# Fetching back and twinning rows of gradients one row per transfer, in parts, in a backward kernel whose end is set by DMA traffic

## The chip, the cores and the metric

The kernel runs on one core of a Trainium2 chip. The metric is device time in microseconds (us). Three timed runs gave 458.6 to 459.25 us, median 459.16. One further execution was profiled: it took 458.38 us, of which the profile's span, from the first to the last instruction of the program, covers 456.6 us.

## The reference, cut to what matters

A one-token decoder network of two block kinds, A (attention over the last 4096 positions of a cache) and B (a dense layer with the mish activation), is run as A, B, A, B with the same weights in both repetitions. The kernel returns the output and the gradients of everything but a bias input that is held constant.

```python
x = A_x                                            # [1, 1, 1024], bf16
x = x + A(layernorm(x), k_cache, v_cache, wq, wo)  # q = x@wq (32 heads of 128, 4 kv heads), softmax over the last 4096 keys, @wo
x = x + B(layernorm(x), w1, b1, w2)                # h = x@w1 + b1 ; h*tanh(softplus(h)) @ w2, inner size 3584
x = x + A(layernorm(x), ...)                       # the same weights again
x = x + B(layernorm(x), ...)
out, vjp = jax.vjp(f, A_x, k_cache, v_cache, wq, wo, w1, b1, w2)
return out, *vjp(grad_out)                         # dk and dv are [1, 4, 32768, 128]: zero but for the last 4096 positions
```

Each weight gradient is a sum of two outer products, one for each repetition (l = 0 and l = 1): for dwo, for example, `dwo[r, c] = oc0[r]*ga0[c] + oc1[r]*ga1[c]`.

## The kernel before, in words

All work is on one core. SyncE (SP in the profile) issues the loads of weights and caches and the stores of the weight gradients; GpSimd (POOL) issues the 56 stores of zeros, 1 MB each, that fill the unused parts of dk and dv (`zeros(n, after)`: POOL first copies one element of a result, so that the n stores start when that result is there). ScalarE (ACT) issues a few small stores. An engine issues in program order.

The forward pass reads the weights as columns. The backward pass goes from block B1 through A1, B0 and A0, and in each block computes the gradient of the block's input. Big weights come through a ring of eight 1 MB slots (`Ring`, line 38): `want` queues a load, and `pump` (line 71 issues it on SP) starts the next one when a slot is released. At the end of B0's backward, `ring.lend(lent)` (line 1119) adds three 1 MB pieces of the tile `W1` that are no longer needed, and the next three loads of wo go there at once. In the profile, tiles whose names begin with W and a number are written `W`, so `W<-W` is a copy inside the tile `W1`.

The weight gradients are made from rows, not columns. The tile `W1` is reused for this: `ROWS` is 128 partitions by 5120 elements of which four pairs of partitions are used, at bases 0, 32, 64 and 96, one pair for each weight gradient (partition base + l for repetition l). Each row holds 1024 elements of one factor and then 3584 or 4096 elements of the other. The columns get there in three ways:

- `rowize` (line 978): TensorE transposes the columns, ACT copies them to SBUF, and for each l one SP transfer (line 986) lays 8 or 32 pieces of 256 bytes into one row. It is called for GB (base 96), GA (base 32) and DQC (base 0). `rowize_f` does the same for DHC (base 64) in 7 pieces of 1024 bytes (line 828).
- `put_by` writes four sets of columns (OC, NA, NB, AC) to small DRAM tensors during the forward pass.
- `take_back` (line 784) fetches them back into `ROWS` in `dn_b0` after its third chunk, at t == 2: one SP transfer for each of the four, 2 rows of 28, 8, 32 and 8 pieces of 256 bytes (line 786). In program order they stand behind `rowize(GB)` and ahead of `rowize_f` and of the three loads of wo that `lend` starts.

`twins` (line 1012), called in the last attention backward at t == 4, copies each pair of rows to a second tile, `TWIN`, at base XOR 32, with one SP transfer for each pair (line 1014): 2 rows of 9216 or 10240 bytes. The twin lets `unit_dw` (line 1016) run the two halves of a 1024-wide unit in two row groups of TensorE. Twins are used only once PSUM has been regrouped in four 1024-wide tiles (`wide`), after the last block's backward.

From there on `work` takes units in turn from four queues: a unit is one or two matmuls of two rows each, an eviction by VectorE (DVE) or ACT (`evac`, lines 305 and 308, which engine by a running sum of costs) into a 1 MB staging buffer, and a store by SP (lines 996 and 1001) when a buffer, or half of one, is full.

Completion of the SP and ACT transfers is counted on eight semaphores that are used in turn (100, 102 to 106, 109 and 110 in the trace). A transfer waits, ahead of its issue, until the earlier transfer on its semaphore has landed.

Of the kernel before, what the change touches and what calls it, by code (L numbers as in the profile page):

```python
# [15 lines left out]
P = 128  # L16
# [77 lines left out]
def kernel(  # L94
# [22 lines left out]
    nc = tc.nc  # L117
# [76 lines left out]
    for hi in range(4):  # L194
        r = slice(32 * hi, 32 * hi + 32)
# [587 lines left out]

    def take_back(name, base, off):
        r = DR[name][:].rearrange("(n l) p -> l n p", l=2)
        nc.sync.dma_start(ROWS[base:base + 2, off:off + r.shape[1] * P].rearrange("l (n p) -> l n p", p=P), r)

    x3, st3, sA1 = attn_fwd(1, x2, st2, False, wo_hook1, last_da)
    put_by("OC", OC, HQ)
# [50 lines left out]
    def dn_b0(g):  # L840
        bcast(lambda c: DHC[:, c, 0:1], STAY)
        mv_open()
        for t in range(TD):
            rowdot(W1[:, t, 0:STAY * P], [LB[0][:, 0:512]], 512, dnp[:, t:t + 1], True)
            mv(W1[:, t, STAY * P:], TF - STAY, TP[:, t:t + 1], lambda i: DHC[:, STAY + i, 0:1], True)
            if t == 2:
                rowize(GB, TD, 96, 0)
                take_back("AC", 96, NOFF)
                take_back("NB", 64, 0)
                take_back("OC", 32, NOFF)  # L850
                take_back("NA", 0, 0)
            if t == 4:
                rowize_f()
        return ln_bwd(dnp, sB0["n32"], sB0["rstd"], g, "B0", lambda k: turn_ahead(("o", 3, 0), ((0,), (1, 2))[k]))
# [110 lines left out]
    ROWS = W1S[:, 0:5120]  # L965
# [7 lines left out]
    TWIN = W1S[:, 11264:16384]  # L973
# [37 lines left out]

    def twins():
        for base, n in ((96, NOFF + F), (64, NOFF + F), (32, NOFF + J), (0, NOFF + J)):
            nc.sync.dma_start(TWIN[base ^ 32:(base ^ 32) + 2, 0:n], ROWS[base:base + 2, 0:n])

    def unit_dw(base, lo, ro, dst, left):

# [135 lines left out]
    def dn1(t):  # L1153
        if t in (3, 6, 7):
            zeros(2 if t == 3 else 1, dnp[:, t:t + 1])
        if t == 4:
            twins()
        if t == 5:
            todo[0].append(units_cols(0, 8, out_4))
# [58 lines left out]
```

## Time and profile before

| | |
|---|---|
| median of three runs | 459.16 us (458.6 to 459.25) |
| the profiled execution | 458.38 us; its span 456.6 us |
| moved by DMA | 183.56 MB, mean 402 GB/s over the span |
| busy share | PE 71%, DVE 56%, ACT 45%, POOL 8% |
| SP's four fetches (line 786) | issued from 280.43 to 282.94 us |
| SP's four twin copies (line 1014) | issued from 321.08 to 327.04 us |
| first eviction from a `wide` tile | 338.70 us |
| last SP store issued | 446.5 us |

Times inside the span are given from its start. In the profile's timeline a row of SP (`SPq`) shows when an issue began and how long SP was held by it; the transfer itself runs later on the core's 16 DMA engines. "DMA share" is the mean busy share of these engines in a stretch. Besides these views, the packed trace holds a record of each DMA packet (start, duration, bytes, queue, but not the engine) and of each semaphore increment by a landing transfer; a time in the text that is said to be from packet or landing records is read there.

### The profile page before, as it was taken

What the parts mean: (1) busy time and instruction counts of PE and PEld (TensorE: products, weight loads), DVE (VectorE), ACT (ScalarE), POOL (GpSimd) and SP (SyncE); (2) the same over time, 40 slices, a digit from 0 to 9 for tenths busy, and PEclk for the clock granted to TensorE, in tenths of its full rate; (3) what the DMA queues carried; (4) which work ended last, traced back from release to release, by engine and by line L of the source; (5) the groups of instructions that cost most, each with busy time, mean ns of one, the idle gap of its engine ahead of it and who ended that gap; (6) DMA issues with size and microseconds to landing.
All of it is one profiled execution on the core that took longest, in us unless ns stands there. A gap on an engine that the chain in (4) does not pass through costs nothing.

```text
span 456.6 us, 13914 instructions
## 1 busy us (share of the span) xinstructions
PE 322.4 (71%) x6225; PEld 258.9 (57%) x6225; DVE 257.5 (56%) x506; ACT 204.6 (45%) x239; POOL 38.5 (8%) x84
## 2 busy tenths in 40 slices
PE   3836543456698898987798868988978988899000
PEld 3735433456597897987798768976922222345000
DVE  4504737278441265846286556763769999989000
ACT  2501001011054277752283542761669999998000
POOL 1000000002031222102100001022130000000000
PEclk9955555555555599978598555995955555555555
DMA  8999999989999999999999979999999999999995
GB/s 334 421 421 421 417 421 419 420 317 422 421 417 423 419 415 416 393 416 418 421 423 425 417 284 342 390 391 420 421 417 420 416 421 419 424 421 418 407 408 227
DMA packets 28377, 183.56 MB, mean 402 GB/s; under 512 B 3706, under 2 KB 3734, under 8 KB 9494
## 3 DMA queue, kind: packets, MB, share of 16 engines
q1 hardware_dynamic: 20162, 123.94, 66.6%
q0 software_dynamic: 8064, 58.72, 31.1%
q8 instruction: 48, 0.79, 0.6%
q14 instruction: 11, 0.09, 0.0%
q10 hardware_dynamic: 92, 0.02, 0.0%
HBM read 83.94 MB, written 98.62 MB: 400 GB/s over the span
## 4 chain that ended last, share of the span: by engine, by line
PE 37%; DMA 28%; DVE 11%; ACT 10%; issue 6%; SPq 0%; ACTq 0%; DVEq 0%
DMA ring<-in_B_w_dram 13%; PE BIG L452 9%; PE TP L471 5%; DMA ring<-in_A_wq_dram 5%; DMA W<-in_A_wo_dram 4%; DMA W<-in_B_w_dram 4%; ACT ring L308 4%; PE wide L1073 4%; PE wide L1022 3%; DVE junk L429 3%; DMA W<-in_A_k_cache_dram 2%; ACT W L308 2%; PE BIG L628 2%; PE MV L648 2%; ACT KT L308 2%
## 5 line engine op out<-in xcount | busy, mean ns | idle before, releaser
L308 ACT COPY ring<-BIG 128x1024 bf16<-128x1024 bf16 x51 | 50.4, 1015 | 45.5 <-PE BIG L452 20.1
L452 PE MATMUL BIG<-ident_bf,ring 128*128 128x128 bf16 x664 | 58.8, 247 | 0.5 <-ACT ring L308 0.3
L1022 PE MATMUL wide<-W 2*128 2x512 bf16 x228 | 52.1, 598 | 9.3 <-ACT W L308 1.9
L452 PEld LDWEIGHTS <-ring 128*128 128x128 bf16 x768 | 55.9, 113 | 1.1 <-issue 0.6
L429 DVE CUSTOM_DVE_ANT_0 junk<-ring,SC 128x1024 bf16<-128x1024 bf16 x32 | 38.9, 1215 | 9.8 <-DMA ring<-in_B_w_dram 9.4
L1022 PEld LDWEIGHTS <-W 2*128 2x128 bf16 x240 | 12.5, 102 | 44.0 <-issue 42.9
L305 DVE CAST ring<-wide 128x1024 bf16<-128x1024 f32 (+1 forms) x29 | 33.7, 1201 | 3.2 <-PE wide L1022 1.4
L471 PEld LDWEIGHTS <-ring 128*128 128x128 bf16 x864 | 30.0, 98 | 7.2 <-issue 3.4
L308 ACT CAST ring<-wide 128x1024 bf16<-128x1024 f32 (+1 forms) x35 | 32.9, 1018 | 1.3 <-PE wide L1073 0.5
L264 POOL DMA_DIRECT2D out_dram<-zt x56 | 29.7, 534 | 37.6 <-DMA out_dram<-zt 37.1
L305 DVE COPY ring<-BIG 128x1024 bf16<-128x1024 bf16 x32 | 21.8, 690 | 17.7 <-PE BIG L452 15.7
L429 DVE CUSTOM_DVE_ANT_0 junk<-ring,DSX 128x1024 bf16<-128x1024 bf16 x24 | 29.4, 1224 | 0.8
L648 PE MATMUL MV<-NB,W 128*128 128x1 bf16 x448 | 16.4, 172 | 14.8 <-DMA W<-in_B_w_dram 12.8
L308 ACT COPY KT<-BIG 128x1024 bf16<-128x1024 bf16 x14 | 13.8, 1008 | 26.7 <-PE BIG L628 25.2
L648 PEld LDWEIGHTS <-W 128*128 128x128 bf16 x448 | 15.8, 118 | 15.6 <-DMA W<-in_B_w_dram 13.4
L514 PE MATMUL MV<-NA,ring 128*128 128x1 bf16 x512 | 15.1, 165 | 12.6 <-DMA ring<-in_A_wq_dram 11.2
L308 ACT COPY W<-BIG 128x1024 bf16<-128x1024 bf16 x21 | 20.7, 1014 | 5.0 <-PE BIG L452 4.4
L452 PE MATMUL BIG<-ident_bf,W 128*128 128x128 bf16 x288 | 22.3, 221 | 0.3 <-issue 0.3
L514 PEld LDWEIGHTS <-ring 128*128 128x128 bf16 x512 | 14.6, 104 | 13.3 <-DMA ring<-in_A_wq_dram 11.9
L305 DVE CAST VS<-wide 128x1024 bf16<-128x1024 f32 (+1 forms) x17 | 19.7, 1188 | 3.6 <-PE wide L1022 3.0
L1073 PE MATMUL wide<-W 32*128 32x256 bf16 x128 | 20.9, 402 | 0.9 <-ACT ring L308 0.8
L308 ACT CAST KT<-wide 128x1024 bf16<-128x1024 f32 x20 | 20.4, 1032 | 1.8 <-PE wide L1022 0.9
(258 smaller groups left out, 538.5 us busy)
## 6 DMA issues: line engine op xcount, KB each, us to landing
out_dram<-zt POOLq DMA_DIRECT2D x56, 1024.0 KB, 20.3
ring<-in_A_wq_dram SPq DMA_DIRECT2D x24, 1024.0 KB
ring<-in_A_wo_dram SPq DMA_DIRECT2D x14, 1024.0 KB
ring<-in_B_w_dram SPq DMA_DIRECT2D x13, 1024.0 KB
W<-in_A_wo_dram SPq DMA_DIRECT2D x10, 1024.0 KB
W<-in_B_w_dram SPq DMA_DIRECT2D x8, 896.0 KB
out_dram<-ring SPq DMA_DIRECT2D x7, 1024.0 KB
out_dram<-ring SPq DMA_DIRECT2D x13, 512.0 KB
```

Source lines behind the costliest of these rows:

```text
L264: nc.gpsimd.dma_start(dst, zt[:])
L305: nc.vector.tensor_copy(dst, src)
L308: nc.scalar.copy(dst, src)
L429: nc.vector.tensor_tensor_reduce(out=out, in0=a, in1=vec, scale=1.0, scalar=acc if i else 0.0, op0=ALU.mult, op1=ALU.add, accum_out=acc)
L452: nc.tensor.transpose(b[:, i * P:(i + 1) * P], block(w, i) if block else w[:, i * P:(i + 1) * P], ident_bf[:])
L471: nc.tensor.matmul(out, lhsT=w[:, i * P:(i + 1) * P], rhs=rhs_of(i), start=fresh[0], stop=last and i == n - 1, skip_group_check=True)
L514: nc.tensor.matmul(q_ps[:, h:h + 1], lhsT=ch[:, h * P:(h + 1) * P], rhs=NA[:, t, l:l + 1], start=(k == 0 and h == 0), stop=(k == TD - 1), ...
L628: nc.tensor.transpose(b[:, i * P:(i + 1) * P], T[:, g, 8 * b8 + i, :], ident_bf[:])
L648: nc.tensor.matmul(h_ps[:, fb:fb + 1], lhsT=f_block(W1[:, t], fb), rhs=NB[:, t, l:l + 1], start=(t == 0 and fb == 0), stop=(t == TD - 1), ...
L1022: nc.tensor.matmul(b[:, 512 * i:512 * i + 512], lhsT=R[at:at + 2, lo:lo + P], rhs=R[at:at + 2, ro + 512 * i:ro + 512 * i + 512], start=Tru ...
L1073: nc.tensor.matmul(b[:, k * 256:(k + 1) * 256], lhsT=RT[32 * g:32 * g + 32, a, tp, :], rhs=YS[32 * g:32 * g + 32, :], start=True, stop=Tru ...
```

## The change

`take_back` issues one transfer for each row, where it issued one for both: eight instead of four. `twins` also issues one transfer for each row, eight instead of four, and cuts each row in 16 pieces (576 or 640 bytes). The outermost dimension of these transfers is then 28, 8, 32, 8 and 16, where it was 2. The bytes, their places and the order among the other steps stay.

```diff
     def take_back(name, base, off):
         r = DR[name][:].rearrange("(n l) p -> l n p", l=2)
-        nc.sync.dma_start(ROWS[base:base + 2, off:off + r.shape[1] * P].rearrange("l (n p) -> l n p", p=P), r)
+        for l in range(2):
+            nc.sync.dma_start(ROWS[base + l:base + l + 1, off:off + r.shape[1] * P].rearrange("o (n p) -> o n p", p=P),
+                              r[l:l + 1])
...
     def twins():
         for base, n in ((96, NOFF + F), (64, NOFF + F), (32, NOFF + J), (0, NOFF + J)):
-            nc.sync.dma_start(TWIN[base ^ 32:(base ^ 32) + 2, 0:n], ROWS[base:base + 2, 0:n])
+            for l in range(2):
+                to = (base ^ 32) + l
+                nc.sync.dma_start(TWIN[to:to + 1, 0:n].rearrange("o (a x) -> o a x", a=16),
+                                  ROWS[base + l:base + l + 1, 0:n].rearrange("o (a x) -> o a x", a=16))
```

## The prediction

> **What bounds the kernel now.** I read the page's slices first, then busy time by stretches, then SP's timeline around the edited lines. In the slices the DMA engines are full nearly throughout, while no compute engine is. (40 slices of 11.4 us.)
>
> ```profile
> DVE  4504737278441265846286556763769999989000
> ACT  2501001011054277752283542761669999998000
> DMA  8999999989999999999999979999999999999995
> GB/s 334 421 421 421 417 421 419 420 317 422 421 417 423 419 415 416 393 416 418 421 423 425 417 284 342 390 391 420 421 417 420 416 421 419 424 421 418 407 408 227
> ```
>
> The stretches show where a microsecond of DMA work that is lost could still be made up. Columns: stretch, its length, busy us and instructions by engine, clock, DMA share, GB/s.
>
> ```profile
> 281.00:285.00 4.00, 4.00 (x93) 4.00 (x91) 2.37 (x12) 0.94 (x1) 0.00 (x0) 0.50 0.99 411
> 285.00:288.00 3.00, 3.00 (x31) 2.66 (x30) 1.80 (x7) 1.43 (x2) 0.00 (x0) 0.56 0.98 304
> 288.00:300.00 12.00, 11.46 (x280) 11.08 (x278) 9.75 (x16) 9.66 (x13) 1.23 (x3) 1.00 1.01 419
> ...
> 365.00:434.00 69.00, 50.22 (x284) 20.46 (x282) 52.11 (x48) 53.26 (x59) 0.00 (x0) 0.50 1.02 419
> 434.00:448.00 14.00, 0.00 (x0) 0.00 (x0) 0.00 (x0) 0.00 (x0) 0.00 (x0) 0.50 1.02 406
> 448.00:450.00 2.00, 0.00 (x0) 0.00 (x0) 0.00 (x0) 0.00 (x0) 0.00 (x0) 0.50 1.02 408
> 450.00:452.00 2.00, 0.00 (x0) 0.00 (x0) 0.00 (x0) 0.00 (x0) 0.00 (x0) 0.50 0.55 223
> 452.00:454.00 2.00, 0.00 (x0) 0.00 (x0) 0.00 (x0) 0.00 (x0) 0.00 (x0) 0.50 0.18 74
> ```
>
> From 288 us to 450 the share stays near 1; compute is over at 434, and stores run on to 455. So the end is the sum of DMA work after 288, and compute that is a few us late is covered by stores still queued. An idle DMA engine before the end is not covered by anything. The last five us are ragged: by the packet records the last engine ends at 454.89, the next at 453.64, 453.53 and 453.17, the earliest near 450.
>
> The edited steps stand here in SP's timeline (start, us held, line, transfer, count), with POOL's zeros on either side:
>
> ```profile
> 278.89 1.43 SPq L986 DMA_DIRECT2D W<-W  x2
> 280.43 0.51 SPq L786 DMA_DIRECT2D W<-dr_AC  x1
> 280.99 0.46 SPq L786 DMA_DIRECT2D W<-dr_NB  x1
> 281.55 0.34 SPq L786 DMA_DIRECT2D W<-dr_OC  x1
> 281.94 1.00 SPq L786 DMA_DIRECT2D W<-dr_NA  x1
> 283.03 1.55 SPq L828 DMA_DIRECT2D W<-W  x2
> 284.69 2.15 SPq L71 DMA_DIRECT2D W<-in_A_wo_dram  x3
> 288.76 1.37 SPq L986 DMA_DIRECT2D W<-W  x2
> ```
> ```profile
> 275.88 1.05 POOL L264 DMA_DIRECT2D out_dram<-zt  x2
> 298.93 1.05 POOL L264 DMA_DIRECT2D out_dram<-zt  x2
> ```
>
> SP goes without a pause from 278.89 to 286.8. The three loads of wo at 284.69 wait for nothing but SP: their last reader in `W1` (the matmuls of `dn_b0`) ended at 282.9. Meanwhile DMA lives on the two zero stores of 275.88. Their landings come at 285.4 to 286.5 on 14 engines (two more at 287.7), and the first packet of the loads starts at 285.76, 1.08 us after its issue. Loads take over as zeros run out, which is the dip to 304 GB/s. POOL's next zeros come at 298.93.
>
> **take_back: SP's time.** Four more issues stand ahead of the loads. Cost from below: 4 at the shortest fetch, 0.34, plus gaps of 0.055: 1.6 us. From above: the nearest rows are those of one row in parts. The pairs of line 986 hold SP 1.43 and 1.37 us for 8 pieces, and the pair of 32 pieces at 319.18 holds it 1.85. Two pairs of 1.85 (AC, OC) and two of 1.40 (NB, NA) make 6.5, with gaps 6.7, against 2.60 before (280.43 to 283.03): 4.1 us. If SP paid by the piece (152 before and after) the cost would be about 0; line 1014 speaks against that, about 1 us each for two pieces. I take the middle of 1.6 and 4.1, 2.9 us, because the pairs of 986 may be held up by one another: the first of the 32-piece pair took 0.50, the second 1.29. `rowize_f` and then the three loads move by it.
>
> **What that is worth.** With nothing queued on either DMA queue between 286 and the loads, a load that is issued 2.9 us later leaves 14 engines idle 2.9 us longer. The two that serve the two-row transfers were late anyhow and lose some 2. Taken together 2.8 us, and since all that follows is full, it stays to the end.
>
> Beside it: the moved loads land, in the landing records, at 290.57, 293.74 and 296.28, and the next ring load at 299.17; TensorE first uses them at 294.66, 296.80, 299.74 and 302.24. The margins are 4.1, 3.1, 3.5 and 3.1 us, so 2.9 hides; past 3.1 the matmuls wait, which delays evictions, not the queued stores. The second `rowize(GA)` pair (288.76, waiting for ACT until 288.74) would leave SP about 1 us later; its rows are first read at 310.9. The ring load of 291.40 slips by some 0.5, behind three loads still in the queue. The loads of wq from 293.58 wait for slots and stay. No step passes POOL's or ACT's queue.
>
> **take_back and twins: DMA engines.** Before, two engines carry each of these transfers: of the 16 increments on a fetch's semaphore, 14 come together at the issue and only two at the landing. By packet records 76 pieces of 256 bytes pass on each in 1.05 us (285.38 to 286.43), and the four twins take 2 x 0.347 + 2 x 0.385 = 1.46 us of each, in a full stretch. After, the fetches lie inside the idle stretch, at no cost. The twins put 8 pieces of some 0.033 us (between 0.018 for 256 bytes and 0.046 for 1024) and 8 end marks of 0.009 on all 16: 0.33 us each, and 1.46 leaves the two. That shortens the end only if the last engine is one of the two, and then by at most 1.25, where the next one ends. I followed packets from the twins to the end (one starts 3 to 4 ns before the one ahead of it on its engine ends): the two seem to end at 452.7 and 453.2, later than most but not last. Threads can be swapped; I give 1 in 3 to the last being one of them. Likeliest: +0.3.
>
> The Trainium skill (DMA: Bandwidth & Descriptors, "Why a DMA increments its semaphore by 16 and not by 1") says a transfer runs on the largest number of engines, up to 16, that divides the outermost sizes of both sides. The two landings agree; by it the new transfers run on 14, 8, 16 and 8 engines and the twins on 16. The same page's rules for kernel authors say to coalesce small transfers, below 64 KB mostly overhead; SP's rows agree, 0.34 to 1.0 us for 4 to 16 KB.
>
> **twins: SP and the wait for them.** Eight issues of about 1 us instead of four: SP leaves near 329.4 (six from 321.08, then the pair of base 0, which waits for `rowize(DQC)`, landed by 326.4) instead of 327.0; its next is the store at 339.74. The twins landed 5.6 to 6 us after their issue, so the last would land near 335.4. The first reader is the wide unit at 338.05. Cost 0, cover 2.6 us; past that evictions wait and use up the 14 us of stores that run on after 434.
>
> **Sum.** 2.8 + 0.3 = +3.1 us on the profiled execution's 458.38 (span 456.6 plus 1.8 around it). The median shown is 0.8 above that execution: 459.16 + 3.1 = 462.3.
>
> **Rivals.**
> 1. Not slower: balance decides and issues are cheap. If SP pays by the piece, the loads stay at 284.7, the two engines lose 1.05 + 1.46 us, and if the last is one of them the end moves by -1.25 + 0.33 = -0.9; where the third and fourth also end earlier, by -1.2. Time 458.0 to 458.6. It decides once SP's delay is under about 0.9 us. For: both engines are late at 287.7 and the twins lie in a full stretch. Against: all rows at lines 786, 828, 986 and 1014 take over 0.3 us, whatever their pieces. Faster 0.08; it shares 0.05 of "same". By itself, the Trainium skill's rule on engines (the same page and section) would do just this.
> 2. Partly cancelled: delay 1.6 and a twin engine last: 1.6 - 0.9 = +0.7, 459.9. "Same", 0.06.
> 3. SP waits as well. Eight semaphores in turn: the second NA fetch needs the second GB row (landed 285.07), and `rowize_f` the AC fetches (286.3 before). By the schedule above SP comes to them at 286 to 287, just past; pieces slower by 1 us make a wait of as much. Delay 4.1 plus 0.5 and late matmuls: 463.5 to 464.2. Chance 0.2.
> 4. The change doesn't do what it says: both sides of a twin are contiguous, and if the pieces were merged again each row would be one packet, all on one engine: 4 x 0.347 + 4 x 0.385 = 2.93 us there instead of 1.46. SP's cost stays: 462 to 463.5. Chance 0.07. (`rowize` keeps its pieces in the trace.)
>
> **Numbers.** My forecast 0.54; the rivals 0.13, 0.06, 0.2 and 0.07. Slower by more than 0.2% (0.92 us, about what a measurement of this kernel can tell from no change): 0.54 + 0.2 + 0.07 = 0.81; same 0.11; faster 0.08. The range goes from just above the unchanged time, 459.4 (the cheap delay with part of the balance), to 464.2 (the dear one with waits); it leaves out most of rival 1 and what lies beyond 3.
>
> **What would show it.** Line 786 with eight issues over 5 to 7 us; the first load of wo at 287 to 289 instead of 284.69; DMA share in 285:288 well under 0.98 and GB/s well under 304; two late landings gone from the zeros; twins on 16 engines, no wait at the wide units; the stores from 340 on at the same rate, ending some 3 us later. Wrong if the loads go out before 285.6, or if the dip grows and the end does not move: then there is slack behind 288 that I don't see, or the last engine was one of the two.

## The result: 0.86% slower, and the profile after

The changed kernel takes 462.71 us (median; 462.62 to 463.44) against 458.82 (458.41 to 459.25) for the kernel before: 3.9 us more, ratio 1.0086, 95% interval 1.0075 to 1.0098. The forecast was 462.3 us, range 459.4 to 464.2, slower. The profiled execution took 462.62 us, span 460.8.

SP's timeline of the changed kernel (start, us held, line, transfer, count) around the edited fetches:

```profile
279.58 1.45 SPq L988 DMA_DIRECT2D W<-W  x2
281.14 1.58 SPq L787 DMA_DIRECT2D W<-dr_AC  x2
282.77 1.29 SPq L787 DMA_DIRECT2D W<-dr_NB  x2
284.16 1.16 SPq L787 DMA_DIRECT2D W<-dr_OC  x2
285.37 1.30 SPq L787 DMA_DIRECT2D W<-dr_NA  x2
287.94 1.54 SPq L830 DMA_DIRECT2D W<-W  x2
289.59 1.31 SPq L71 DMA_DIRECT2D W<-in_A_wo_dram  x3
290.99 1.37 SPq L988 DMA_DIRECT2D W<-W  x2
292.47 0.39 SPq L71 DMA_DIRECT2D ring<-in_A_wo_dram  x1
```

The eight fetches hold SP for 5.33 us where four held it for 2.31. Then there is a gap that the kernel before doesn't have, from 286.67 to 287.94. SP's waits in this stretch (278 to 300 us; line, what was waited for, us in total, times, longest) name it, first in the changed kernel, then in the kernel before:

```profile
SPq L830 <- DMA W<-dr_AC: 1.2, 1, 1.2
```
```profile
SPq L71 <- DMA W<-dr_AC: 0.2, 1, 0.2
```

The row of the kernel before is a wait of its third wo load for the AC fetch. Line 830 (`rowize_f`) reads nothing that the AC fetch writes. Its first transfer is the ninth, counted from the first AC fetch, and takes the completion semaphore of the first AC fetch, number 103; by the landing records that fetch, issued at 281.14, landed at 287.87. So the first wo load goes out at 289.59, not 284.69: 3.0 us from the issues, 1.2 from this wait, and 0.7 since SP's row of transfers began that much later in this execution (279.58 against 278.89).

Busy time by stretches in the changed kernel (stretch, length, busy us by engine, clock, DMA share, GB/s):

```profile
281.00:285.00 4.00, 4.00 (x92) 3.79 (x90) 2.44 (x11) 1.00 (x1) 0.00 (x0) 0.50 1.01 417
285.00:288.00 3.00, 3.00 (x31) 2.87 (x28) 2.38 (x9) 1.01 (x1) 0.00 (x0) 0.54 0.57 214
288.00:290.00 2.00, 1.60 (x26) 1.41 (x25) 0.80 (x2) 1.16 (x2) 0.00 (x0) 1.00 0.02 5
...
365.00:434.00 69.00, 51.11 (x289) 20.55 (x284) 53.01 (x48) 54.20 (x60) 0.00 (x0) 0.50 1.01 418
```

```profile
454.00:456.00 2.00, 0.00 (x0) 0.00 (x0) 0.00 (x0) 0.00 (x0) 0.00 (x0) 0.50 0.83 332
456.00:458.00 2.00, 0.00 (x0) 0.00 (x0) 0.00 (x0) 0.00 (x0) 0.00 (x0) 0.50 0.19 78
458.00:460.00 2.00, 0.00 (x0) 0.00 (x0) 0.00 (x0) 0.00 (x0) 0.00 (x0) 0.50 0.04 14
```

From 288 to 290 us the DMA engines do next to nothing, while TensorE goes on. The stretches from 365 us on run at the old rate, and the last engine ends some 4 us later, at 459.15 instead of 454.89 by the packet records. Over 285:293, the kernel before first:

```profile
285.00:293.00 8.00, 7.66 (x139) 7.19 (x138) 5.49 (x13) 5.11 (x6) 0.00 (x0) 0.84 0.99 372
285.00:293.00 8.00, 7.60 (x134) 7.29 (x132) 5.60 (x14) 4.62 (x6) 0.00 (x0) 0.83 0.51 173
```

At the full stretches' 420 GB/s that is 8 x 199 / 420 = 3.8 us of DMA work not done, close to the 3.9 us of the medians. The packet records show that it is not made up. Summed from the start of the span, the changed kernel is behind the kernel before by 0.8 us of DMA work at 285 us (the later start), 4.5 at 293, 4.6 at 300 and at 400, and 4.5 at 450.

### The profile page after: what moved, and what is told of

Read it like the earlier page. It is cut to its first block, busy times and chain, and to the rows that moved or that the text cites. A ratio compares the mean times of both kernels' runs of the same rounds, so it can differ in the third digit from the quotient of the medians.

```text
span 460.8 us, 13926 instructions
## 1 busy us (share of the span) xinstructions
PE 321.3 (70%) x6225; PEld 257.1 (56%) x6225; DVE 257.7 (56%) x506; ACT 204.8 (44%) x239; POOL 38.5 (8%) x84
## 4 chain that ended last, share of the span: by engine, by line
PE 37%; DMA 32%; DVE 9%; ACT 8%; issue 6%; DVEq 0%; SPq 0%; ACTq 0%
DMA ring<-in_B_w_dram 13%; PE BIG L452 9%; DMA ring<-in_A_wq_dram 6%; DMA W<-in_A_wo_dram 6%; PE TP L471 5%; DMA W<-in_B_w_dram 4%; PE wide L1027 4%; ACT ring L308 4%; PE wide L1078 3%; DMA W<-in_A_k_cache_dram 2%; PE BIG L628 2%; PE MV L648 2%; ACT W L308 2%; DVE VS L305 2%; PE MV L911 2%
## 5 line engine op out<-in xcount | busy, mean ns | idle before, releaser
L452 PE MATMUL BIG<-ident_bf,ring 128*128 128x128 bf16 x664 | 56.3, 240 | 0.6 <-ACT ring L308 0.4
L452 PEld LDWEIGHTS <-ring 128*128 128x128 bf16 x768 | 54.1, 110 | 1.3 <-issue 0.9
L471 PEld LDWEIGHTS <-ring 128*128 128x128 bf16 x864 | 29.5, 97 | 7.3 <-issue 3.9
L514 PEld LDWEIGHTS <-ring 128*128 128x128 bf16 x512 | 14.8, 104 | 13.8 <-DMA ring<-in_A_wq_dram 12.1
```

Source lines behind the costliest of these rows:

```text
L452: nc.tensor.transpose(b[:, i * P:(i + 1) * P], block(w, i) if block else w[:, i * P:(i + 1) * P], ident_bf[:])
L471: nc.tensor.matmul(out, lhsT=w[:, i * P:(i + 1) * P], rhs=rhs_of(i), start=fresh[0], stop=last and i == n - 1, skip_group_check=True)
L514: nc.tensor.matmul(q_ps[:, h:h + 1], lhsT=ch[:, h * P:(h + 1) * P], rhs=NA[:, t, l:l + 1], start=(k == 0 and h == 0), stop=(k == TD - 1), ...
```

## The experiments

Theory A: more issues on SP, and waits for semaphores used in turn, send the wo loads out late; the DMA queues run empty; nothing behind makes it up. Rivals: the twins carry the loss (B); the outer dimension itself costs (C); late loads hold up compute (D). In the table, "missing" is 8 x (372 - GB/s in 285:293) / 420, the DMA work that each profile lacks there against that of the kernel before. Until its twins at 321 us e2 runs the program of the kernel before, so its 0.5 us show how much this column can differ by chance. The ratio is not that of the medians: in e5 it makes 3.5 us and not 3.9.

| kernel | ratio to before, interval | change of the median, us | GB/s in 285:293 | missing, us |
|---|---|---|---|---|
| changed | 1.0086, 1.0075 to 1.0098 | +3.9 | 173 | 3.8 |
| e1 fetches only | 1.0057, 1.0045 to 1.0069 | +2.6 | 207 | 3.1 |
| e2 twins only | 1.0006, 0.9997 to 1.0015 | +0.3 | 346 | 0.5 |
| e3 fetches in halves, two rows each | 1.0049, 1.0036 to 1.0063 | +2.3 | 205 | 3.2 |
| e4 changed, two zeros moved ahead | 1.0011, 0.9999 to 1.0023 | +0.8 | 365 | 0.1 |
| e5 changed again | 1.0077, 1.0063 to 1.0091 | +3.9 | 161 | 4.0 |
| e6 AC and OC by rows | 1.0042, 1.0029 to 1.0054 | +1.8 | 265 | 2.0 |
| e7 changed, fetches at chunks 3 to 6 | 1.0131, 1.0114 to 1.0148 | +5.9 | 399 | none |
| e8 before, fetches at chunks 3 to 6 | 1.0189, 1.0174 to 1.0203 | +8.5 | 394 | none |
| e9 changed, fetches behind the loads | 1.0187, 1.0167 to 1.0207 | +9.0 | 385 | none |
| e10 before, fetches behind the loads | 1.0091, 1.0075 to 1.0107 | +4.3 | 388 | none |
| e11 before, one zero moved ahead | 0.9987, 0.9978 to 0.9997 | -0.8 | 387 | none |

The missing work follows the time at which the first wo load goes out, counted from POOL's issue of the two zero stores that DMA lives on until then: 8.8 us in the kernel before (284.69 - 275.88), 9.4 in e2, 11.2 in e6, 12.5 in e1 and e3, 13.0 in the changed kernel and in e5. The column "missing" rises in the same order.

**e1 and e2, each part alone.** The diff of the change, its first or its second half.

> Only take_back is changed (eight one-row fetches), the twins stay as before. Theory A (SP issues eight fetches and then waits for the semaphore of the first AC fetch, the three wo loads go out some 4.2 us later, the DMA queues run empty, nothing makes it up): 3.5 to 4.2 us over the kernel before, the first wo load near 289, DMA share in 285:288 near 0.57. Rival B (the 16-piece twins, in a full stretch, carry the loss: 128 more packets and 12 us of SP): within 0.5 us of the kernel before.

> Only the twins are changed. Theory A: between -1.0 and +0.5 us against the kernel before; +0.3 if the last DMA engine is not one of the two that carried the two-row twins, about -0.9 if it is. Rival B: +3 us or more, with the first wide units or stores later than in the kernel before.

Fetches alone cost 2.6 us, less than the 3.5 to 4.2 expected, twins alone 0.3 with an interval that includes none. B is out. The wo loads go out at 288.72 in e1, after two waits of line 830 for the two AC fetches, of 0.5 and 0.2 us, and the missing work is smaller to match.

```profile
SPq L830 <- DMA W<-dr_AC: 0.7, 2, 0.5
```

**e3, as many issues, the outer dimension still 2.**

```diff
-        nc.sync.dma_start(ROWS[base:base + 2, off:off + r.shape[1] * P].rearrange("l (n p) -> l n p", p=P), r)
+        h = r.shape[1] // 2
+        for i in range(2):
+            nc.sync.dma_start(ROWS[base:base + 2, off + i * h * P:off + (i + 1) * h * P].rearrange("l (n p) -> l n p", p=P),
+                              r[:, i * h:(i + 1) * h])
```

> Each fetch is issued as two transfers of half the pieces but of both rows, so there are eight issues, the outer dimension is still 2, and the number of pieces is that of before; twins as before. Theory A (issues cost, not pieces or engines): 2.5 to 4.2 us slower, SP held some 5 us by line 786 and the first wo load at 287.5 to 289.5. Rival C (the outer dimension, that is the number of engines and their completions, costs): within 0.7 us of the kernel before.

+2.3 us, just under the range expected, and about the loss of e1 with the same number of issues, on two engines and not 8 to 16. So the loss doesn't need the outer dimension, and C is out as its cause. That doesn't make the outer dimension free of cost for SP: an issue is cheaper here (the four rows below hold SP 4.0 us, 0.5 of it a wait, against 5.33), but SP waits more. Its timeline and its waits (278 to 300 us):

```profile
281.84 1.22 SPq L788 DMA_DIRECT2D W<-dr_AC  x2
283.11 1.06 SPq L788 DMA_DIRECT2D W<-dr_NB  x2
284.21 0.75 SPq L788 DMA_DIRECT2D W<-dr_OC  x2
286.05 0.96 SPq L788 DMA_DIRECT2D W<-dr_NA  x2
287.29 2.26 SPq L831 DMA_DIRECT2D W<-W  x2
289.66 1.32 SPq L71 DMA_DIRECT2D W<-in_A_wo_dram  x3
```
```profile
SPq L788 <- DMA W<-W: 1.6, 2, 1.1
```

The seventh and eighth fetch stand still for 1.1 and 0.5 us until the two GB rows, whose semaphores they take, have landed.

**e4, the empty stretch filled.** The changed kernel with `zeros(4, dh0)` for `zeros(2, dh0)` and `zeros(3, g0)` for `zeros(5, g0)`.

> The changed kernel, with two of the 1 MB zero stores moved from the end of the last backward (five become three) to the start of dn_b0 (two become four), so that POOL's queue has about 5 us more to move while SP is behind. SP's issues stay as late as in the changed kernel. Theory A (the loss is an empty DMA queue): the hole at 286:290 is filled and the time falls by 3.5 to 4.5 us, to within 1 us of the kernel before. Rival D (the late loads hold up the matmuls, and the compute chain sets the end): within 0.7 us of the changed kernel, or slower since the loads now share the engines with zeros.

```profile
281.81 2.00 SPq L787 DMA_DIRECT2D W<-dr_AC  x2
283.86 2.08 SPq L787 DMA_DIRECT2D W<-dr_NB  x2
286.04 2.08 SPq L787 DMA_DIRECT2D W<-dr_OC  x2
288.17 1.57 SPq L787 DMA_DIRECT2D W<-dr_NA  x2
289.83 1.52 SPq L830 DMA_DIRECT2D W<-W  x2
291.47 1.91 SPq L71 DMA_DIRECT2D W<-in_A_wo_dram  x3
```

SP is later than ever, the loads at 291.47, and yet 3.1 of the 3.9 us are back (3.5 to 4.5 were expected). So late loads cost by the empty queue; D is out as the cause. The hole at 286:290 is filled: 412 GB/s in 285:288 and 433 in 288:290, against 304 and 418 in the kernel before, 0.8 us of DMA work more. Behind it a shallower one opens when the four zeros run out and the loads, issued at 291.47, are only starting:

```profile
290.00:292.00 2.00, 2.00 (x58) 2.00 (x56) 1.60 (x3) 1.28 (x2) 0.00 (x0) 1.00 0.83 320
292.00:300.00 8.00, 6.46 (x148) 6.37 (x144) 4.71 (x9) 5.62 (x6) 0.00 (x0) 0.88 0.96 366
```

The kernel before moves 410 and 421 GB/s there, so 0.4 + 1.0 us of work are missing; less the 0.8 gained, that is 0.6 us, near the 0.8 that is left. The column "missing" ends at 293 and doesn't see most of it. Matmuls wait for the late loads here too (1.5 us, TensorE busy for 6.46 of the 8 us against 7.67 in e1), but the account closes without them. e11 below shows that a zero store moved ahead helps the kernel before as well; against that one e4 is 1.5 us slower.

**e5, the changed kernel again.**

> The changed kernel once more, on the chip of the next three runs, since fetches alone (+2.6 us) and twins alone (+0.3) don't add up to its +3.9. If the rest is run-to-run difference in SP's wait for the first AC fetch (1.2 us in the changed kernel's profile, 0.5 in that of the fetches alone, and the program is the same up to the twins): 461.0 to 462.5 us, not 462.7. If the two parts aid each other: 462.5 or more.

462.92 us, +3.9 once more by the medians, above the 461.0 to 462.5 of the first case. The two parts together cost 1 us more than their sum; from the three intervals of the table I estimate 0.2 to 1.9 us for this gap. That the parts aid each other isn't shown: the difference is already in 285:293 (3.8 and 4.0 us missing, 3.1 in e1), where both programs have issued the same, so it isn't the twins' own transfers. Nor is it the wait for the AC fetch. In this profile there is none: by the landing records the first AC fetch lands at 287.32, before SP comes to line 830. The loads still go out as late, because the issues themselves hold SP longer:

```profile
281.35 1.58 SPq L787 DMA_DIRECT2D W<-dr_AC  x2
282.98 1.93 SPq L787 DMA_DIRECT2D W<-dr_NB  x2
285.01 1.21 SPq L787 DMA_DIRECT2D W<-dr_OC  x2
286.26 1.29 SPq L787 DMA_DIRECT2D W<-dr_NA  x2
287.65 2.04 SPq L830 DMA_DIRECT2D W<-W  x2
289.81 1.31 SPq L71 DMA_DIRECT2D W<-in_A_wo_dram  x3
```

From the first fetch to the first load SP takes 8.45 and 8.46 us in the two profiles of the changed kernel, and 7.92 in that of e1. Why it takes half a microsecond longer there stays open, and with one profile of e1 chance isn't excluded.

**e6, half of the split.** AC and OC by rows, NB and NA as before: six issues.

```diff
+        m = 1 if name in ("AC", "OC") else 2
+        for l in range(0, 2, m):
+            nc.sync.dma_start(ROWS[base + l:base + l + m, ...], r[l:l + m])
```

> Only AC and OC are fetched one row at a time, so there are six issues in place of four; NB, NA and the twins as before. Theory A: two issues at 0.65 to 0.8 us each and no wait for a semaphore, since the tenth transfer then reuses that of the first GB row, long landed: +1.2 to +1.7 us, the first wo load at 286 to 287. A theory in which the loss comes with the wait for a completion alone: within 0.4 us of the kernel before.

+1.8 us; I had expected up to 1.7, with no wait. There was one: the first wo load, at 288.43, takes the semaphore of the first AC fetch, and by the records SP's wait ended at 288.37, when that fetch landed (288.36). (The list of waits names a copy by VectorE instead, but that ended at 288.40.) Without it the load could have gone out at 287.6 at the earliest. I had counted the turn wrongly by one.

**e7 and e8, fetches between later loads.** The calls of `take_back` leave `dn_b0`; in `do1`:

```diff
+        if 3 <= c <= 6:
+            take_back(*(("AC", 96, NOFF), ("NB", 64, 0), ("OC", 32, NOFF), ("NA", 0, 0))[c - 3])
```

> The changed kernel, with the four calls of take_back moved from dn_b0 into the next block's do1, one each at chunks 3 to 6, so that the eight issues stand behind the three wo loads and between the wq loads, where SP has pauses of about a microsecond. Theory A: the first wo load goes out near 284, the hole at 286:290 is gone, and the time falls by 3.5 to 5 us, to 457.7 to 459.0 us. Rival (one-row fetches cost by themselves, wherever they are): 461 us or more.

> The kernel before with the same move: four two-row fetches at chunks 3 to 6. Theory A: 457.5 to 458.7 us, that is 0.2 to 1.2 us faster than the kernel before, since the dip at 285:288 (0.8 us of lost DMA work) shrinks; and within 0.7 us of the changed kernel with the move. If the outer dimension of the fetches were worth something where SP has time, the changed kernel with the move would be the faster of the two by more than that.

Both expectations fell. The hole was gone as expected (399 and 394 GB/s in 285:293), and both kernels were slower than either original. SP's waits from 290 to 312 us, in e7, then in e8:

```profile
SPq L71 <- DMA out_dram<-W: 7.3, 1, 7.3
```
```profile
SPq L786 <- DMA out_dram<-W: 9.0, 2, 8.5
```

`out_dram<-W` is a small store that ACT issues at 300 us or later. In the kernel before, ACT's two stores use semaphores 105 and 109, which SP doesn't need again before 319 us. With the fetches moved, one of them shares a number with an SP transfer that would be ready some 7 us earlier, and stands before it in the turn. All behind it on SP waits, the other fetches too, and TensorE then waits for their rows (from 305 to 330 us of e7):

```profile
PEld L1023 <- DMA W<-dr_OC: 9.6, 1, 9.6
```

By then POOL's zeros, which follow the matmuls, are late as well: those of 317.82 in the kernel before come at 327.37 in e7 and at 330.52 in e8, and in e8 the DMA share from 320 to 330 us is 0.34. That e7 is the faster of the two by 2.6 us would speak for the outer dimension by the sign named above, but with waits and zeros this different the pair doesn't decide it.

**e9 and e10, fetches right behind the three loads.** The four calls follow `ring.lend(lent)`.

> The changed kernel with the four calls of take_back moved right behind the three wo loads (behind lend, ahead of rowize(GA)). If only SP's issue time ahead of these loads counts, the loads go out near 284.1 and the time is that of the kernel before or 0.8 us under it. If the turn of eight semaphores counts as well: the sixth to eighth fetch wait for the three loads to land (some 290, 293 and 295.5), SP comes to the next ring load at 297 to 298 and to the wq loads at 298 to 299 in place of 293.6, the hole moves to 295:299, and the time is 2 to 4 us over the kernel before.

> The kernel before with the same move. Its four fetches take the semaphores of transfers landed by about 287, the second GA row and the next ring load those of the first two loads (290, 293), the first wq load that of the third (295.5), when DMA still has the ring load to move: no hole. The dip at 285:288, 0.8 us of DMA work, shrinks: 0.3 to 0.9 us faster than the kernel before, 457.9 to 458.8 us. If the move harms in any other way: slower than the kernel before.

e9 was to lose 2 to 4 us and lost 9.0; e10 was to win and lost 4.3. The loads went out early (285.59 and 284.17) and the dip was gone. SP's waits from 284 to 312 us, e9 first:

```profile
SPq L787 <- DMA out_dram<-W: 6.4, 1, 6.4
SPq L787 <- DMA W<-in_A_wo_dram: 4.8, 3, 2.0
```
```profile
SPq L71 <- DMA out_dram<-W: 9.5, 2, 7.2
SPq L982 <- DMA W<-in_A_wo_dram: 3.5, 2, 1.7
SPq L786 <- DMA W<-in_A_wo_dram: 3.1, 1, 3.1
```

The foreseen waits, fetches behind the loads' semaphores, are there (4.8 us in e9), and so is the hole (DMA share 0.34 in 294:298 of e9). What I hadn't seen is the same store of ACT: in e10 it holds the first wq load until 304.20, and the DMA engines stand half idle (stretch, ..., DMA share, GB/s):

```profile
295.00:300.00 5.00, 4.81 (x126) 4.66 (x124) 4.14 (x7) 4.57 (x6) 0.68 (x2) 1.00 0.49 163
```

I had read the turn off the order of issue; ACT's stores hold places in it ahead of SP transfers that are ready before them. A move that frees the turn as well wasn't tried.

**e11, the dip of the kernel before filled.** `zeros(3, dh0)` and `zeros(4, g0)`: one zero store moved ahead, the rest as before.

> The kernel before, with one 1 MB zero store moved from the end of the last backward (five become four) to the start of dn_b0 (two become three). It fills the dip at 285:288: 0.2 to 0.9 us faster than the kernel before if the zeros don't hold up the wo loads past their first use (margins of 3.1 to 4.1 us); no faster, or slower, if they do, or if the zeros are missed later between 315 and 343 us.

458.11 us against 458.88: 0.8 us less, about the dip, with an interval just below 1. It has the lowest median here.

## Why the prediction was right, point by point

- **The bound.** Right: DMA work after 288 us sets the end. 3.8 us not done at 285:293 is 3.9 us at the end, and putting other work in that place gives most of it back (e4).
- **Four more issues.** Right: sized at 2.9 us between 1.6 and 4.1, measured 3.0 (5.33 against 2.31). Other executions of the same steps put it at 2.8 to 3.7: the two-row fetches hold SP 2.53 us in e2, the one-row fetches 6.01 in e5. The doubt that kept the value off the upper end was justified: AC and OC took 1.58 and 1.16, not the 1.85 of the 32-piece pair.
- **Semaphores in turn.** The term that the sum lacks. That the wo loads "wait for nothing but SP" was already not quite so: in the kernel before the third of them waits 0.2 us for the AC fetch. More waits stood as the third rival, chance 0.2, "just past". They came: 1.2 us here, 0.7 in e1, 1.6 in e3, none in e5, where issues took longer instead. So the first load is 4.2 us late beyond the later start of the row, not 2.9, and 3.8 us of DMA work are lost, not 2.8.
- **The forecast time.** 462.3 is nearer to 462.71 than the working deserves: it starts from 459.16, and the median of the kernel before came out at 458.82. The change was forecast at 3.1 us and measured at 3.9.
- **Margins of the loads.** The rule was right, the margins were used up. The loads land at 294.45, 297.56 and 300.89, 3.8 to 4.6 us later than before, and past some 3.1 us the matmuls were to wait. They do, a little (288 to 306 us, no such row in the kernel before):

```profile
PEld L452 <- DMA W<-in_A_wo_dram: 0.7, 2, 0.5
PE BIG L452 <- DMA W<-in_A_wo_dram: 0.3, 1, 0.3
```

TensorE's busy time from 288 to 300 is nearly unchanged, 11.38 us against 11.46, and the lag in DMA work doesn't grow after 293, so it cost nothing at the end. The wq loads, which were to stay, did not: three go out at 294.54, 297.64 and 300.98 instead of 293.58, 295.52 and 297.02, each when the wo load that has its semaphore has landed.
- **Twins.** +0.3 forecast, +0.3 in e2, but e2's interval of -0.1 to 0.7 us can't tell this from zero, so the agreement is luck in part. It does exclude the -0.9 of a last engine that carries the twins. SP's share was too small: eight issues took 11.9 us, 1.2 to 1.7 each and not 1. They landed 6.3 to 7.7 us after their issue (5.8 to 6.2 before, where the prediction read 5.6 to 6), the last at 339.56, behind the first wide unit (338.61) and not 2.6 us ahead of it. No wide unit waited for one; the cover that was to explain this was gone.
- **The engines.** The two late engines were misread. In the second zero store they still land last, at 288.51 and 288.78, the 14 others by 287.33, though the fetches no longer run on two engines. Something else makes them late. The tail stays ragged: by the landing records of the last store, the earliest engine is 4.2 us ahead of the last, 5.1 in the kernel before.
- **The count of engines.** The AC fetch's semaphore now climbs in 14 steps. So the rule in the Trainium skill (DMA: Bandwidth & Descriptors, "Why a DMA increments its semaphore by 16 and not by 1") holds here too; e2 and e3 show no gain from it in this place. The fourth rival is out: the twins' packets are of 576 and 640 bytes, 64 of each, and 16 landings belong to each twin.

## What to carry to other kernels

Where the end is a sum of DMA work, look at what each engine's queue issues next, and behind what: the price of a small transfer is paid by the large one behind it, once the queues run dry. Count the transfers between reuses of a completion semaphore before adding or moving one, other engines' transfers included; a landed predecessor costs nothing, one that hadn't landed cost 0.2 to 8.5 us here. Work that is free to move, such as stores of zeros, covered such a place (e4, e11) where each of the four reorderings tried here lost.

## What was not expected of the hardware

- The time for which an issue holds SP is not set by the transfer alone: the same eight fetches took 5.33 us in the changed kernel, 6.01 in e5, which is the same program, and 7.73 in e4 with two more zeros queued, while the two-row fetches of e10 took 0.24 to 0.71 each and those of the kernel before 0.34 to 1.00. It is not just how full the DMA engines are: in e9 (share 0.99 in 285:293) the first three fetches took 0.79, 0.75 and 0.61 us, in the changed kernel 0.78, 0.75 and 0.64. What sets it stays open.
- A small transfer beside full queues lands late: the first AC fetch of 7 KB took 6.7 us from issue to landing, and the 14 KB fetch of the kernel before 5.9. In the changed kernel's profile that is more than eight issues take, which is why the ninth waits; in e5 it took 6.0, and the ninth didn't wait.
